# A fused attention and gated feed-forward kernel: first weight chunk loaded first, exponents guarded by a scaled absolute value, two buffers for the first product, and new planned times for the queues

## The chip, the cores and the metric

The kernel runs on one core of a Trainium2 chip. The metric is device time in microseconds (us) of one execution; smaller is better. Five engines work side by side, each through its own queue in order: TensorE (PE: matrix products; PEld is its loading of weights), VectorE (DVE), ScalarE (ACT), GpSimd (POOL), and SyncE (SP), which here issues all transfers (DMA) between the device memory and the on-chip memory.

## The reference

Attention over a causal window of 64 positions, then a feed-forward block with a gate that comes from a convolution over three positions:

```python
scores = scale * np.matmul(q, k.transpose(0, 1, 3, 2))      # 8 batches, 8 heads, 576 positions, 64 wide
mask = (rel >= 0) & (rel < 64)
scores = np.where(mask, scores, -1e9)
attn = np.exp(scores - scores.max(-1))
attn = attn / (attn.sum(-1) + 1e-09)
x = np.matmul(attn, v)                                      # heads side by side: 512 wide
h = np.maximum(x @ w_in, 0.0)                               # 512 -> 1024
conv_out = sum(conv_w[k] * hp[:, k:k + S] for k in range(3))
gate = 1 / (1 + np.exp(-conv_out))
out = (h * gate) @ w_out                                    # 1024 -> 512
```

q, k and v are float32; w_in, conv_w and w_out are float64.

## The kernel before

All 4608 positions (8 batches of 576) are cut into 12 units of 384 positions (NX), u = 0 to 11. For each unit the kernel computes:

- **scores**: twelve blocks in three batches b of four blocks each (`qk`), then the row maximum (`row_max`), the exponential (`exps`), a guard of the sums, a reciprocal and the normalising (`normalise`). In units 0 and 1 the blocks are 128 columns wide and TensorE transposes the result (`transpose_pe`, `untile`); from unit 2 on they are 96 wide, VectorE transposes, and transfers put the result in place.
- **values** (`values`, four column blocks c), split into a high part `xh` and a low part `xl` (`split_hi`, `split_lo`).
- **the first product** (`mm1`), for f = 0 to 7, blocks of 128 of the 1024 columns: three matmuls for high and low parts, for each of four c, so 12 calls for an f; then `relu` into `hbuf`.
- **the gate**: `conv_mid` on ScalarE, two `conv_side` on VectorE, `sig`, `gate`, `gate_hi` and `gate_lo`, for pairs of f.
- **the second product** (`mm2`), 12 calls for an f, into four accumulators `po`; at the unit's end these are copied and stored.

The weights come as float64 and are turned into a high and a low float32 part on the chip, once, in the first 100 us. They arrive as raw 32-bit words in chunks (`weights`, `to_f32`): ScalarE takes the absolute value of the high words (L248) and scales the low words (L255); GpSimd clamps at 2^-15 from below (L249, with TINY); VectorE shifts and masks (L250), puts the sign back (L252) and adds the low word (L256); then GpSimd (L273, for w_in) or ScalarE (L271, for w_out) rounds to the high part, and VectorE subtracts for the low part (L274). w_in comes as two chunks of one f and three of two, w_out as four of two.

The order of the instructions is made by a planner. Each piece of work is put on a list with `at(t, engine, cost, do, r, w)`: t is its planned place, in steps of one f (unit u starts at 8u), and r and w are what it reads and writes. `queued` goes through the list with costs written by hand and, for each engine, takes the ready piece with the smallest t. The instructions are then issued in that order, each engine's queue in order. So every number in the table START and every cost moves instructions on all queues. Where the planner sees TensorE idle in the first 110 us it puts in dummy matmuls on the zero tile `spare` (`keep_busy`, L212).

The raw words lie in a tile that is later used for the transposed scores and the output (`flat`, named T in the profile); `w24` (w in the profile) holds the converted chunk. `hbuf` is one buffer, so the relu of a unit must wait for the gate of the unit before.

Of the kernel before, what the change touches and what calls it, by code (L numbers as in the profile page):

```python
# [8 lines left out]
F32 = mybir.dt.float32  # L9
# [7 lines left out]
W = 64  # L17
# [11 lines left out]
LAG = 5  # L29
# [4 lines left out]
TINY = 2.0 ** -15  # L34
# [26 lines left out]
def queued(works, fill=None):  # L61
# [22 lines left out]
    free = {"PE": 0.0, "DVE": 0.0, "ACT": 2.0, "POOL": 0.7, "SP": 1.3}  # L84
    state = dict.fromkeys(free)
    waiting = {e: [] for e in free}
# [5 lines left out]
    while left:  # L92
# [17 lines left out]
        if fill and e == "PE" and start < FILL_TO:  # L110
            t = max(free[e], FILL_FROM)
            n = int((start - t) * FILL)
# [10 lines left out]
        if x.mb:  # L123
            dma = max(dma, start) + x.mb * 2.7
            end = dma + 1.9
        for k in x.r + x.w:
            if k in touched:
                touched[k] = e, end
# [12 lines left out]
    "v0": -34.213,  # L141
    "pv0": -15.486,
    "conv": -34.622,
    "bits": ((-44.162, -48.108), (-49.962, -46.523)),
    "qk1": -44.058,
    "v1": -6.318,
    "qk2": 0.918,
    "qk0": (-88.698, -55.197, -55.435),
    "ex0": (-38.484, -35.539, -25.91),
    "sc1": (-35.664, -14.916, -14.661),  # L150
    "ex1": (-10.948, -3.722, -2.234),
    "mask": -13.894,
    "sig": ((5.143, 6.743, 8.637, 10.624), (2.954, 4.077, 7.59, 9.996), (4.046, 6.806, 8.285, 10.314)),
    "in": (-40.063, -38.679, -33.327, -12.569, -5.818),
    "out": (-5.241, -4.847, 7.996, 9.148),
# [8 lines left out]
FILL, FILL_FROM, FILL_TO = 4.0, 2.0, 110.0  # L164
# [3 lines left out]
def attention_moe(ctx: ExitStack, tc: tile.TileContext, q, k, v, w_in, conv_w, w_out, out):  # L168
# [10 lines left out]
    hbuf = pool.tile([P, NF, NG + 2], F32, name="hbuf")  # L179
# [17 lines left out]
    bits = [flat.bitcast(U32)[:, 4 * DM * i:4 * DM * (i + 1)].rearrange("p (e two) -> p e two", two=2) for i in range(2)]  # L197
    T_BITS = (0,), (0, 1)
    w24 = many(2, [P, 2 * DM], F32, "w24")
# [26 lines left out]
    def load_qk(t, u, gs=(0, 1)):  # L226

        for g in gs:
            c, n = slice(2 * g, 2 * g + 2), (4, 2)[g] * W
            cut = (0, n + W, NX + W), (0, n, NX)  # L230
            for a in ((0, 1), (1, 2)) if u == 0 else ((0, 2),):
                for name, sb, dram, ends in (("k", ks, k, cut[0]), ("q", qs, q, cut[1])):
                    e = slice(ends[a[0]], ends[a[1]])
                    at(t, "SP", 0.7, lambda c=c, e=e, sb=sb, dram=dram: nc.sync.dma_start(sb[:, c, e], dram[u, :, c, e]),
                       w=[(name, g, i) for i in range(*a)], mb=0.00105 * (e.stop - e.start))

    def load_v(t, u):
        for g in range(2):
            c = slice(2 * g, 2 * g + 2)
            at(t, "SP", 0.7, lambda c=c: nc.sync.dma_start(vs[:, c], v[u, :, c]), w=[("v", g)], mb=0.79)  # L240
# [3 lines left out]
    def to_f32(t, n, st, x, kb, kt):  # L244
# [3 lines left out]
        at(t, "ACT", 0.0009 * n + 0.2, lambda: nc.scalar.activation(x, hw.bitcast(F32), AF.Abs), r=kb, w=kt)  # L248
        at(t, "POOL", 0.0027 * n + 0.02, lambda: nc.gpsimd.tensor_scalar(x, x, TINY, None, op0=ALU.max), w=kt, port=PORT_CL)  # L249
        two(t, "DVE", 0.00052 * n + 0.06, lambda: nc.vector.tensor_scalar(  # L250
            xu, xu, 3, 0x3FFFFFF8, op0=ALU.logical_shift_left, op1=ALU.bitwise_and), w=kt)
        two(t, "DVE", 0.00104 * n + 0.07, lambda: nc.vector.scalar_tensor_tensor(  # L252
            xu, hw, 0xC0000000, xu, op0=ALU.bitwise_and, op1=ALU.bitwise_or), r=kb, w=kt)
# [4 lines left out]
    def weights(t, src, fs, hi, lo, key, buf, halves):  # L258
# [4 lines left out]
        for f, a, tl in zip(fs, halves, load_at(buf, halves, t)):  # L263
            at(tl, "SP", 0.7, lambda f=f, a=a: nc.sync.dma_start(
                bits[buf][:, a * DM:(a + 1) * DM], src[f].bitcast(U32).rearrange("p (e two) -> p e two", two=2)),
               w=[("bits", buf, a)], mb=0.52)
        n = len(fs) * DM
        to_f32(t, n, st, x, kb, kt)
        his, los = [f"{key}{f}h" for f in fs], [f"{key}{f}l" for f in fs]
# [24 lines left out]
    def weights_conv(t_load, t):  # L294
        at(t_load, "SP", 0.7, lambda: nc.sync.dma_start(
# [40 lines left out]

# [397 lines left out]
```

## Time and profile before

| | us |
|---|---|
| median of 3 runs | 527.84 (527.21 to 528.04) |
| span of the profiled execution | 525.6 |
| PE busy | 516.8 (98%) |
| PEld busy | 499.1 (95%) |
| ACT busy | 384.7 (73%) |
| DVE busy | 377.9 (72%) |
| POOL busy | 105.2 (20%) |

The page gives no time for the profiled execution but its span, from the first to the last instruction; the runs' median is 2.2 us above it. The shares are averages over a prologue, in which weights are converted and the first scores are computed, and ten units or so that repeat at some 40 us each. A busy TensorE may be busy with dummy matmuls: these are told by their line, L212. The granted clock is 1.00 throughout.

### The profile page before, as it was taken

The page shows a single profiled execution, that of the slowest core. Times are in us where ns is not written, and L with a number is a line of the kernel's source. Part 1 is how long each engine was busy: PE and PEld are TensorE (multiplying, and loading weights), DVE is VectorE, ACT ScalarE, POOL GpSimd, SP SyncE. Part 2 cuts the span into 40 slices and gives each one's busy share as a digit, 9 for nine tenths or more (in the row PEclk, how much of TensorE's full clock was granted, in tenths as well). Part 3 has the DMA queues.
Part 4 walks back from the last instruction along what each step waited for, and adds up shares of the span by engine and source line. Part 5 has one row for each costly group of instructions (what it writes and reads, how often), then busy time and mean ns, then how long its engine had stood idle before and what let it go on. Part 6 is the DMA issues. An engine that isn't in the chain of part 4 may idle for free.

```text
span 525.6 us, 14814 instructions
## 1 busy us (share of the span) xinstructions
PE 516.8 (98%) x5814; PEld 499.1 (95%) x5814; DVE 377.9 (72%) x1084; ACT 384.7 (73%) x1017; POOL 105.2 (20%) x192
## 2 busy tenths in 40 slices
PE   9999899999999999999999999999999999999996
PEld 8988899999899999999999999999999999999996
DVE  3899999987667775677668667767767767645552
ACT  2999999796895984795795796697687687544541
POOL 6754663112120210120111011021021021000000
PEclk9999999999999999999999999999999999999999
DMA  8982850282472264272272173173083053010011
GB/s 285 382 287 92 265 221 1 72 304 81 136 253 54 68 218 117 68 275 64 67 268 68 61 259 76 44 289 78 16 301 85 10 178 83 13 61 0 2 60 61
DMA packets 29461, 69.97 MB, mean 133 GB/s; under 512 B 5712, under 2 KB 17616, under 8 KB 29392
## 3 DMA queue, kind: packets, MB, share of 16 engines
q1 hardware_dynamic: 29392, 69.03, 39.8%
q8 instruction: 46, 0.75, 0.6%
q14 instruction: 23, 0.19, 0.1%
HBM read 47.73 MB, written 9.47 MB: 109 GB/s over the span
## 4 chain that ended last, share of the span: by engine, by line
PE 90%; DVE 8%; issue 1%; ACT 0%
PE po L567 39%; PE acc L504 36%; PE acc L484 6%; PE sc L353 5%; PE acc L212 3%; DVE s L360 1%; DVE c L538 1%; DVE w L256 1%; DVE w L252 1%; DVE wil L274 1%; DVE s L381 1%; DVE w L250 1%; DVE xl L491 1%; PE po L353 0%; DVE cw L252 0%
## 5 line engine op out<-in xcount | busy, mean ns | idle before, releaser
L538 DVE SCALAR_TENSOR_TENSOR c<-hbuf,cw,c 128x386 f32<-128x386 f32 (+1 forms) x192 | 110.0, 624 | 32.9 <-ACT c L531 32.7
L567 PE MATMUL po<-gh,woh 128*128 128x386 f32 (+1 forms) x384 | 132.4, 345 | 0.0
L504 PE MATMUL acc<-xh,wih 128*128 128x384 f32 x384 | 131.1, 341 | 0.8 <-POOL sm L373 0.8
L567 PE MATMUL po<-gh,wol 128*128 128x386 f32 (+1 forms) x384 | 129.8, 338 | 0.0
L567 PE MATMUL po<-gl,woh 128*128 128x386 f32 (+1 forms) x384 | 129.8, 338 | 0.0
L504 PE MATMUL acc<-xh,wil 128*128 128x384 f32 x384 | 129.8, 338 | 0.0
L504 PE MATMUL acc<-xl,wih 128*128 128x384 f32 x384 | 129.7, 338 | 0.0
L370 ACT ACTIVATE s<-s,nm 128x96 f32<-128x96 f32 (+2 forms) x288 | 105.2, 369 | 6.5 <-DVE nm L360 6.3
L558 DVE TENSOR_TENSOR gl<-c,gh 128x772 fp32r<-128x772 f32 (+1 forms) x48 | 55.0, 1146 | 28.1 <-ACT gh L554 27.7
L567 PEld LDWEIGHTS po<-gh,woh 128*128 128x128 f32 x384 | 72.2, 188 | 2.9
L504 PEld LDWEIGHTS acc<-xh,wih 128*128 128x128 f32 x384 | 72.1, 188 | 2.4 <-POOL sm L373 1.0
L381 POOL TENSOR_TENSOR s<-s,r 128x768 f32<-128x768 f32 x27 | 39.7, 1471 | 165.6 <-DVE r L376 154.3
L550 DVE TENSOR_TENSOR c<-c,hbuf 128x772 f32<-128x772 f32 (+1 forms) x48 | 47.0, 981 | 35.9 <-ACT c L545 35.9
L567 PEld LDWEIGHTS po<-gl,woh 128*128 128x128 f32 x384 | 72.3, 188 | 0.0
L567 PEld LDWEIGHTS po<-gh,wol 128*128 128x128 f32 x384 | 72.3, 188 | 0.0
L504 PEld LDWEIGHTS acc<-xh,wil 128*128 128x128 f32 x384 | 72.2, 188 | 0.0
L504 PEld LDWEIGHTS acc<-xl,wih 128*128 128x128 f32 x384 | 72.1, 188 | 0.0
L525 ACT ACTIVATE hbuf<-acc 128x384 f32<-128x384 f32 x64 | 30.9, 486 | 44.6 <-PE acc L504 44.4
L545 ACT ACTIVATE c<-c 128x772 f32<-128x772 f32 (+1 forms) x48 | 40.7, 847 | 27.4 <-DVE c L538 27.2
L360 DVE CUSTOM_DVE_ANT_0 s<-sc,mask 128x96 f32<-128x96 f32 (+2 forms) x272 | 51.5, 255 | 11.0 <-POOL mask L321 7.0
L370 ACT ACTIVATION_READ_ACCUMULATOR s<-s,nm 128x1 f32 x288 | 54.7, 190 | 0.0
L531 ACT ACTIVATE c<-hbuf,cw 128x386 f32<-128x386 f32 (+1 forms) x96 | 53.6, 609 | 0.0
(64 smaller groups left out, 603.5 us busy)
## 6 DMA issues: line engine op xcount, KB each, us to landing
v<-in_v_dram SPq DMA_DIRECT2D x24, 768.0 KB, 7.3
ub<-T SPq DMA_DIRECT2D x240, 48.0 KB, 1.9
k<-in_k_dram SPq DMA_DIRECT2D x22, 448.0 KB, 5.3
q<-in_q_dram SPq DMA_DIRECT2D x22, 384.0 KB, 6.3
out_dram<-T SPq DMA_DIRECT2D x8, 772.0 KB, 4.4
T<-in_w_in_dram SPq DMA_DIRECT2D x8, 512.0 KB, 6.0
T<-in_w_out_dram SPq DMA_DIRECT2D x8, 512.0 KB, 5.3
out_dram<-T SPq DMA_DIRECT2D x3, 768.0 KB, 6.4
```

Source lines behind the costliest of these rows:

```text
L360: nc.vector.tensor_tensor_reduce(out=ss[b][:, i, h, o:n], in0=banks_of(u, b)[h][:, i * P + o:i * P + n], in1=mask[m][:, o:n], scale=-0.125 ...
L370: nc.scalar.activation(x, x, AF.Exp, bias=nms[b][:, e], scale=-1.0, accum_out=sms[b][:, e])
L381: on.tensor_tensor(sv, sv, rs[b].unsqueeze(2).broadcast_to([P, 2 * NB, n]), ALU.mult)
L484: nc.tensor.matmul(acc[bank(("v", u, c))][h * D:(h + 1) * D, t * W:(t + 1) * W], vs[:, c, t, h], ub[g][:, 2 * p:2 * p + 2, 2 * t + h], sta ...
L504: nc.tensor.matmul(acc[bank(("m", u, f))][:, :NX], w[:, f, c], x[u % 2][:, c], start=(c == 0 and j == 0), stop=(c == NC - 1 and j == 2))
L525: nc.scalar.activation(hbuf[:, f, o:o + NX], ps[:, :NX], AF.Relu)
L531: nc.scalar.activation(cs[i % 2][:, a, :n], hbuf[:, f, 1:1 + n], AF.Copy, scale=cw[:, 1, f:f + 1])
L538: nc.vector.scalar_tensor_tensor(c, hbuf[:, f, e:e + n], cw[:, e, f:f + 1], c, op0=ALU.mult, op1=ALU.add)
L545: nc.scalar.activation(c, c, AF.Sigmoid)
L550: nc.vector.tensor_tensor(c, c, hbuf[:, 2 * i:2 * i + 2, 1:1 + n], ALU.mult)
L558: nc.vector.tensor_tensor(gls[ring(u, i)][:, :, :n], cs[i % 2][:, :, :n], ghs[ring(u, i)][:, :, :n].bitcast(F32), ALU.subtract)
L567: nc.tensor.matmul(po[o][:, :n], w[:, f, es], x, start=(f == 0 and j == 0), stop=(f == NF - 1 and j == 2))
```

## The change

Four things are changed.

First, the conversion has no clamp any more: Abs gets a scale of 2^-112, and the shift and the sign are adapted, so that the chain goes from ScalarE to VectorE without GpSimd. Second, the raw words get a tile of their own (`bits`), and the converted chunks lie in T. Third, `hbuf` becomes two buffers, by u % 2. Fourth, the planner gets other rules and numbers: SyncE is taken as free from 0.75, an issue costs less, dummy matmuls are planned from 1.2 at 2.2 a microsecond up to the sixth, the scores and row maxima of wide blocks are planned in halves and blocks, the lag of the second product behind the first is a table instead of 5, and START is new nearly throughout; among it, the first chunk of w_in and the convolution's weights are loaded ahead of q and k.

```diff
-LAG = 5
-TINY = 2.0 ** -15
...
-    free = {"PE": 0.0, "DVE": 0.0, "ACT": 2.0, "POOL": 0.7, "SP": 1.3}
+    free = {"PE": 0.0, "DVE": 0.0, "ACT": 2.0, "POOL": 0.7, "SP": 0.75}
...
-            n = int((start - t) * FILL)
+            n = int((start - t) * (FILL if start > COLD else 2.2))
...
-    "bits": ((-44.162, -48.108), (-49.962, -46.523)),
+    "bits": ((-210.989, -90.898), (-76.132, -86.24)),
+    "lag": (5.734, 4.983, 5.01, 5, 4.601, 6.631),
...
-    hbuf = pool.tile([P, NF, NG + 2], F32, name="hbuf")
+    hbufs = many(2, [P, NF, NG + 2], F32, "hbuf")
...
-    bits = [flat.bitcast(U32)[:, 4 * DM * i:4 * DM * (i + 1)].rearrange("p (e two) -> p e two", two=2) for i in range(2)]
-    w24 = many(2, [P, 2 * DM], F32, "w24")
+    bits = many(2, [P, 2 * DM, 2], U32, "bits")
+    w24 = [flat[:, 8 * NT * 32:8 * NT * 32 + 2 * DM], flat[:, 16 * NT * 32:16 * NT * 32 + 2 * DM]]
...
-        at(t, "ACT", 0.0009 * n + 0.2, lambda: nc.scalar.activation(x, hw.bitcast(F32), AF.Abs), r=kb, w=kt)
-        at(t, "POOL", 0.0027 * n + 0.02, lambda: nc.gpsimd.tensor_scalar(x, x, TINY, None, op0=ALU.max), w=kt, port=PORT_CL)
-        two(t, "DVE", 0.00052 * n + 0.06, lambda: nc.vector.tensor_scalar(
-            xu, xu, 3, 0x3FFFFFF8, op0=ALU.logical_shift_left, op1=ALU.bitwise_and), w=kt)
+        at(t, "ACT", 0.0009 * n + 0.2, lambda: nc.scalar.activation(x, hw.bitcast(F32), AF.Abs, scale=2.0 ** -112), r=kb, w=kt)
+        two(t, "DVE", 0.00052 * n + 0.06, lambda: nc.vector.tensor_scalar(xu, xu, 3, None, op0=ALU.logical_shift_left), w=kt)
         two(t, "DVE", 0.00104 * n + 0.07, lambda: nc.vector.scalar_tensor_tensor(
-            xu, hw, 0xC0000000, xu, op0=ALU.bitwise_and, op1=ALU.bitwise_or), r=kb, w=kt)
+            xu, hw, 0x80000000, xu, op0=ALU.bitwise_and, op1=ALU.bitwise_or), r=kb, w=kt)
...
     def carry(u, fs):
+        hbuf = hbufs[u % 2]
...
-            nc.gpsimd.tensor_copy(hbuf[:, fs, :2], hbuf[:, fs, e:e + 2])
+            nc.gpsimd.tensor_copy(hbuf[:, fs, :2], hbufs[(u - 1) % 2][:, fs, e:e + 2])
...
-                at(n + LAG + 0.5 + 0.01 * o, "PE", 0.53, lambda f=f, o=o: mm2(u, f, o),
+                at(n + START["lag"][min(u, 5)] + 0.5 + 0.01 * o, "PE", 0.53, lambda f=f, o=o: mm2(u, f, o),
...
-    nc = bacc.Bacc("TRN2", target_bir_lowering=False, num_devices=1)
+    nc = bacc.Bacc("TRN2", target_bir_lowering=False, num_devices=1, dynamic_dma_scratch_size=1024)
```

The new code is longer, so lines get new numbers: dummy matmuls L212 become L214, scores L353 become L356, row maxima L360 become L363, the conversion's L248 and L250 become L250 and L251 (L252, L255, L256, L271, L273 and L274 keep theirs), normalising L381 becomes L384, transposes L387 become L390, values L484 become L495, the first product L504 becomes L515, the second L567 becomes L580.

How the order of the instructions moves, at three places, and by counts at a fourth. SyncE's queue at its start, before:

```order
L234 DMA k<-in_k_dram 128x2x320
L234 DMA q<-in_q_dram 128x2x256
L234 DMA k<-in_k_dram 128x2x128
L234 DMA q<-in_q_dram 128x2x128
L234 DMA k<-in_k_dram 128x2x192
...
L234 DMA k<-in_k_dram 128x2x256
L234 DMA q<-in_q_dram 128x2x256
L264 DMA T<-in_w_in_dram 128x1024 x4
```

and after:

```order
L264 DMA bits_102<-in_w_in_dram 128x1024
L295 DMA cbits<-in_conv_w_dram 128x48
L236 DMA k<-in_k_dram 128x2x320
L236 DMA q<-in_q_dram 128x2x256
L236 DMA k<-in_k_dram 128x2x128
...
L236 DMA q<-in_q_dram 128x2x256
L264 DMA bits_102<-in_w_in_dram 128x1024
L264 DMA bits_103<-in_w_in_dram 128x1024 x2
```

One chunk of w_in and the convolution's weights stand ahead of the first k and q; the other three chunks stay behind these.

VectorE's queue from the first batch's reciprocal on, in unit 0 (s_80 and s_81 are the first two batches before), before:

```order
L250 TENSOR_SCALAR w_101<-w_101 128x512
L252 SCALAR_TENSOR_TENSOR w_101<-T,w_101 128x512
L376 RECIPROCAL r_89<-sm_86 128x8
L381 TENSOR_TENSOR s_80<-s_80,r_89 128x1024
L250 TENSOR_SCALAR w_101<-w_101 128x512
L256 ISA w_101<-T,w_101 128x1024
L252 SCALAR_TENSOR_TENSOR w_101<-T,w_101 128x512
...
L256 ISA w_101<-T,w_101 128x1024
L274 TENSOR_TENSOR wil<-w_101,wih 128x512
L376 RECIPROCAL r_90<-sm_87 128x8
L381 TENSOR_TENSOR s_81<-s_81,r_90 128x1024
L274 TENSOR_TENSOR wil<-w_101,wih 128x512
```

and after (where these batches are s_81 and s_82; the first chunk's L251 and L252 stand at the very front of the queue, its L256 and L274 between the first row maxima):

```order
L379 RECIPROCAL r_90<-sm_87 128x8
L256 ISA cw<-cbits,cw 128x48
L384 TENSOR_TENSOR s_81<-s_81,r_90 128x1024
L251 TENSOR_SCALAR T<-T 128x512
L379 RECIPROCAL r_91<-sm_88 128x8
L252 SCALAR_TENSOR_TENSOR T<-bits_102,T 128x512
L384 TENSOR_TENSOR s_82<-s_82,r_91 128x1024
L256 ISA T<-bits_102,T 128x1024
L274 TENSOR_TENSOR wil<-T,wih 128x512
```

The second batch's normalising has moved ahead of the row maxima of unit 1, and L274 of the second chunk stands right behind its L256, with the rounding L273 on GpSimd between them.

TensorE's queue where unit 0 is transposed for the first time, before:

```order
L212 MATMUL acc_106<-spare 128x112 x28
...
L387 MATMUL po_108<-ident,s_80 128x128 x4
L387 MATMUL po_109<-ident,s_80 128x128 x4
L212 MATMUL acc_106<-spare 128x112 x8
...
L212 MATMUL acc_106<-spare 128x112 x7
L387 MATMUL po_110<-ident,s_81 128x128 x4
L387 MATMUL po_111<-ident,s_81 128x128 x4
L212 MATMUL acc_106<-spare 128x112 x3
L484 MATMUL acc_106<-ub_61,v 64x64 x12
```

(sixteen scores of unit 1 stand in each of the two gaps) and after:

```order
L214 MATMUL acc_107<-spare 128x112 x15
L390 MATMUL po_109<-ident,s_81 128x128 x4
L390 MATMUL po_110<-ident,s_81 128x128 x4
L214 MATMUL acc_107<-spare 128x112 x3
L390 MATMUL po_111<-ident,s_82 128x128 x4
L390 MATMUL po_112<-ident,s_82 128x128 x4
L214 MATMUL acc_107<-spare 128x112 x3
L495 MATMUL acc_107<-ub_61,v 64x64 x12
```

The scores of unit 1 have moved behind the first values. Over the whole queue there are 99 dummy calls before and 63 after; ahead of the first scores there are 12 before and 20 after.

TensorE's queue where the second product for f = 6 and 7 of unit 0 begins has, ahead of that place, 174 calls of the first product, 96 of the values and 128 narrow scores (four batches of 32) before, and 180, 120 and 160 after.

151 lines of the change are left out of this document (84 added, 67 removed), and 6 rows, old and new, of the table START.

## The prediction

> **What bounds the kernel now.** I read the stages first, then TensorE's waits, then the dummy matmuls, then VectorE up to the last converted weight. The columns of the stage rows are length, then busy time of PE, PEld, DVE, ACT and POOL, granted clock, DMA share, GB/s.
>
> ```profile
> 0.00:36.71 36.71, 34.70 (x536) 32.44 (x537) 26.92 (x120) 26.52 (x100) 23.86 (x62) 1.00 0.88 317
> 36.71:65.44 28.73, 26.34 (x358) 24.40 (x358) 28.70 (x67) 26.58 (x64) 14.41 (x10) 1.00 0.59 194
> 65.44:113.60 48.16, 48.04 (x527) 46.66 (x524) 46.05 (x124) 43.01 (x100) 15.52 (x20) 1.00 0.38 124
> 234.00:274.40 40.40, 40.40 (x483) 39.07 (x482) 28.57 (x88) 30.55 (x83) 5.77 (x11) 1.00 0.40 132
> ```
> ```profile
> PE sc L353 <- DVE nm L360: 1.3, 2, 0.9
> PE acc L212 <- DVE spare L215: 1.0, 1, 1.0
> PE po L387 <- DVE s L381: 0.9, 2, 0.7
> PE acc L504 <- POOL sm L373: 0.8, 1, 0.8
> PE acc L484 <- DVE xl L491: 0.5, 1, 0.5
> ```
> From the third stage on TensorE is busy nearly without a gap, and a unit in the middle has no gap at all: there the arithmetic of TensorE alone sets the time, and VectorE and ScalarE have a quarter free. All waits of TensorE, 4.5 us, lie before 65.44. In the second stage VectorE is busy for 28.70 of 28.73 us. So the prologue is set by VectorE, and TensorE fills its holes with dummy matmuls (L212), which look busy and are worth nothing:
>
> ```profile
> 0.00:65.44 65.44, 27.40 (x198) 25.66 (x198) 1.00 0.75 263
> 1.05 5.46 PE L212 MATMUL acc<-spare 128*128 128x112 f32 x24 [1.05 <-DVE spare L215]
> 6.44 1.38 PE L353 MATMUL sc<-k,q 64*64 64x64 f32 x32
> 7.75 1.15 PE L212 MATMUL acc<-spare 128*128 128x112 f32 x8
> 11.64 6.50 PE L212 MATMUL acc<-spare 128*128 128x112 f32 x56
> 44.37 1.16 PE L353 MATMUL sc<-k,q 64*32 64x96 f32 x64 [0.32 <-DVE nm L360]
> 55.62 1.62 PE L484 MATMUL acc<-ub,v 128*64 128x64 f32 x48
> 97.48 5.81 PE po L567 x33
> 118.90 2.13 PE po L567 x12
> ```
> Only what TensorE does in vain, 27.40 + 4.5 = 31.9 us, can be won. The question is how early VectorE lets it stop. The last thing that VectorE must give is the low half of the last output-weight chunk (L274, at 95.54 below); TensorE needs it for the row at 97.48, the second product for f = 6 and 7 of the first unit, before which stand 72 calls of that product.
>
> **The sum, on VectorE.** I counted the instructions that the order puts up to that L274. Before and after they are the same kinds and counts but for three: 8 more row maxima of 96 columns, one normalising of 768 columns and one reciprocal fewer. So VectorE's time to this point changes by its start, by its waits, and by how long the same instructions take.
>
> ```profile
> 0.00:96.67 96.67, 85.71 (x241) 1.00 0.61 212
> 8.00 0.23 DVE L360 CUSTOM_DVE_ANT_0 s<-sc,mask 128x64 f32<-128x64 f32 x1 [7.00 <-POOL mask L321]
> 14.54 0.43 DVE L250 TENSOR_SCALAR w<-w 128x512 uint32<-128x512 uint32 x1 [1.00 <-POOL w L249]
> 16.06 1.52 DVE L381 TENSOR_TENSOR s<-s,r 128x1024 f32<-128x1024 f32 x1
> 22.37 1.40 DVE L381 TENSOR_TENSOR s<-s,r 128x1024 f32<-128x1024 f32 x1
> 28.68 2.06 DVE L381 TENSOR_TENSOR s<-s,r 128x1024 f32<-128x1024 f32 x1
> 40.62 1.22 DVE L381 TENSOR_TENSOR s<-s,r 128x1024 f32<-128x1024 f32 x1
> 21.54 0.69 DVE L274 TENSOR_TENSOR wil<-w,wih 128x512 fp32r<-128x512 f32 x1
> 23.69 1.52 DVE L274 TENSOR_TENSOR wil<-w,wih 128x512 fp32r<-128x512 f32 x1
> 57.22 0.68 DVE L250 TENSOR_SCALAR w<-w 128x1024 uint32<-128x1024 uint32 x1
> 62.87 1.21 DVE L250 TENSOR_SCALAR w<-w 128x1024 uint32<-128x1024 uint32 x1
> 52.53 0.24 DVE L360 CUSTOM_DVE_ANT_0 s<-sc,mask 128x96 f32<-128x96 f32 x1
> 53.95 1.14 DVE L538 SCALAR_TENSOR_TENSOR c<-hbuf,cw,c 128x386 f32<-128x386 f32 x2
> 39.45 1.02 DVE L252 SCALAR_TENSOR_TENSOR cw<-cbits,cw 128x24 uint32<-128x24 uint32 x1
> 95.54 1.22 DVE L274 TENSOR_TENSOR wol<-w,woh 128x1024 fp32r<-128x1024 f32 x1
> 27.90 3.50 POOL L249 TENSOR_SCALAR w<-w 128x1024 f32<-128x1024 f32 x1 [1.17 <-ACT w L248]
> 18.59 1.00 POOL L273 CAST wih<-w 128x512 fp32r<-128x512 f32 x1 [1.20 <-DVE w L256]
> 12.24 0.68 ACT L248 ACTIVATE w<-T 128x512 f32<-128x512 f32 x1 [3.21 <-DMA T<-in_w_in_dram]
> ```
> - **The clamp leaves GpSimd** (one of 3.50 us stands above). VectorE ran on beside it, but some instructions were drawn out: the normalisings by 0.30, 0.18 and 0.84 against 1.22, L274 by 0.83, L250 by 0.53, and the tiny L252 by some 0.9. That is 3.6 us, plus the wait of 1.00 at 14.54. The scale in ScalarE's Abs makes no new instruction, and one arithmetic step fewer in L250 I price at 0; if the row went by steps it would be at most half of 0.68 in each, some 2.5 us over the nine.
> - **The first chunk comes first.** Its steps L250 and L252 on VectorE (some 1.3 us with the small ones for the convolution) move into the time ahead of the row maxima, in which VectorE waited 7 us. ScalarE's wait of 3.21 goes too.
> - **The first scores come later.** Twenty dummy calls stand ahead of them instead of twelve. Each call is two rows: twelve took 5.39 (1.05 to 6.44), and the next went at 1.07 for four (7.75 to 8.82), so twenty end at 1.05 + 5.39 + 2.14 = 8.6. The chunk and the small load push q back, but not beyond that:
>
> ```profile
> 1.24 0.46 SPq L234 DMA_DIRECT2D q<-in_q_dram  x1
> q<-in_q_dram SPq DMA_DIRECT2D x1, 256.0 KB, 3.4
> T<-in_w_in_dram SPq DMA_DIRECT2D x1, 512.0 KB, 6.2
> T<-in_w_in_dram SPq DMA_DIRECT2D x1, 512.0 KB, 6.9
> ```
>   q landed at 4.6. Two issues of half a microsecond and one chunk (the second of two issued 0.5 apart lands 1.2 later) put it at some 6.9. With about 1.0 for the scores at the later rate and the 0.25 that passed from 7.75 to 8.00, the row maxima start at 9.8 instead of 8.00.
> - **A new wait.** For the second chunk L256 and L274 now stand next to each other, with GpSimd's L273 (1.00) between them: VectorE waits some 1.3 us, and its row maxima stand behind it. Before, other work stood there. Bounds: 0 (if VectorE is late anyway) and 2.6 (both small chunks); I take 1.3.
>
> Busy time without the first memset (0.17) is 85.5; it becomes 85.5 - 3.6 - 1.3 + 0.4 = 81.0. The 0.4 is 1.4 for eight row maxima (52.53 to 53.95) less some 1.0 for the small normalising (three quarters of 1.22) and the reciprocal. VectorE's other waits between 8.00 and 96.67 were 88.67 - 85.54 - 1.00 = 2.1; I keep them and add 1.3. The last low half is then ready at 9.8 + 81.0 + 3.4 = 94.2 instead of 96.7.
>
> **The sum, on TensorE.** By its row at 97.48 TensorE had done 174 calls of the first product, 72 of the second, 96 of the values and four score batches of 32 calls. With the second h buffer the order lets unit 1 run further ahead: ahead of the same row stand 180, 72, 120 and five. That is 3.7 us of useful work more (6 calls at 2.13 for twelve; 24 calls of the values, 48 rows, at 1.55, since what follows the row at 55.62 starts at 57.17; a batch at 1.1). TensorE gets there at 94.2 + 0.2 = 94.4 instead of 97.48, so it is 97.48 - 94.4 + 3.7 = 6.8 us ahead. The same from the other side: 99 dummy calls become 63, of which 20 cost 7.5 and 43 at 6.43 / 28 cost 9.9, so 17.4 instead of 27.4; of the 10.0 saved, 3.2 come back as waits on VectorE that nothing fills.
>
> **What costs nothing.** From 65.44 TensorE waits for nothing, so the new lags and places of units 2 and later reorder a full engine: 0 either way, with up to a microsecond lost if a half comes late. The copies across the two h buffers and one more small memset lie on GpSimd, busy 5.77 of 40.40. GpSimd issues no transfer of data in the trace, so the smaller scratch for its descriptors changes nothing but room. The end (after 521.3) is unchanged.
>
> The page gives 525.6 us of span for the profiled execution and no other time; the median of the runs lies 2.2 above it. The forecast is 527.84 - 6.8 = 521.0.
>
> **A rule against the trace.** The POOL row at 27.90 lasts 3.50 us, and in it VectorE's L381 took 2.06 instead of 1.22. The Trainium skill, page SBUF — State Buffer, section Who interferes with whom, has it that a GpSimd instruction and a VectorE instruction with two SBUF inputs exclude each other for the whole of the one that came first. By that rule L381 could not end before 31.40; the trace has it end at 30.74, so the lock is not whole here. By the rule each of nine clamps would hold VectorE for its length, the time would fall by far more, and the third rival below would be the case.
>
> **Rivals.**
> 1. VectorE gains little: its waits grow from 3.4 to 6 or 7, since the row maxima hang on scores which TensorE, in order, issues behind transposes and values that wait for VectorE again. For it: the list of waits runs both ways. Against it: in the second stage VectorE had 0.03 us without work. Then 97.5 for the last half, and 527.84 - (97.48 - 97.7 + 3.7) = 524.4.
> 2. Slower. The first scores are 2.1 us later (8.6 for 6.44), and everything of the softmax chain with them; if the clamps had cost VectorE only what it had to spare, nothing pays that back, and the cast adds 1.3. The price is 2.1 + 1.3 = 3.4, so 531.2. It decides where the normalising of the third batch of unit 0 starts later than 28.68 + 2. Against it: the wait of 1.00 and the 0.84 lie on just that chain.
> 3. VectorE is freed further, and TensorE is bound by its own order: waits of VectorE vanish, or the clamps' cost was larger. TensorE's useful work to its row is 65.6 + 3.7 = 69.3; with 17.4 of dummies and 1.05 at the start it gets there at 87.7, and the time is 527.84 - (97.48 - 87.7 + 3.7) = 514.4. Half way from the forecast, 517.7, is likelier.
>
> **Chances.** Forecast (gain of 3.6 to 9.8) 0.72, first rival 0.10, third 0.10, no change 0.03, slower 0.05. Two tenths of a per cent, 1.05 us, is about what this kernel's runs (527.21 to 528.04) can tell from no change. Faster is 0.92, same 0.03, slower 0.05. The range takes the forecast's bounds, 527.84 - 9.8 = 518.0 and 527.84 - 3.4 = 524.4: waits of VectorE of 0.4 and 6.8.
>
> **What would show it.** The first scores at 8.5 to 8.8 and the first row maximum near 9.8; no L249 on GpSimd; normalisings of 1024 columns within 1.3; an L274 of 512 columns waiting for L273; L212 at 17 to 18 us in all; the last low half at 92 to 96; a middle unit still at 40.2. Wrong would be a wait of TensorE after 100, or row maxima that wait for scores by more than 2 us in sum.

## The result, and the profile after

The changed kernel takes 520.0 us (median of 4 runs, 519.84 to 520.37) against 527.91 for the kernel before (4 runs, 527.21 to 528.04): a ratio of 0.9845, interval 0.9812 to 0.9878. That is 7.9 us less; 6.8 were forecast. The profiled execution took 519.87 us, its span is 517.9 us, and before's was 525.6. One execution of e12_rows_in_line below took 1271.6 us and is left out of all its numbers.

The stages of after, cut as those of before (length, then busy time of PE, PEld, DVE, ACT and POOL, granted clock, DMA share, GB/s):

```profile
0.00:36.71 36.71, 33.16 (x457) 30.14 (x458) 25.71 (x123) 28.19 (x106) 16.04 (x57) 1.00 0.87 311
36.71:65.44 28.73, 27.16 (x466) 24.49 (x466) 27.97 (x85) 25.48 (x61) 7.50 (x18) 1.00 0.71 266
65.44:113.60 48.16, 47.41 (x513) 44.94 (x513) 46.31 (x107) 41.23 (x84) 5.38 (x13) 1.00 0.32 96
234.00:274.40 40.40, 40.40 (x484) 39.07 (x483) 27.29 (x87) 30.04 (x83) 6.13 (x11) 1.00 0.41 136
```

The picture is the same as before: TensorE has no gap in a middle unit, and VectorE has few in the second stage. GpSimd fell from 23.86 to 16.04 and from 14.41 to 7.50 us. What TensorE does in vain is next, the dummies (now L214), then the start of the program and the row that needs the last low half:

```profile
0.00:65.44 65.44, 18.31 (x126) 16.50 (x126) 1.00 0.80 291
```
```profile
1.05 6.24 PE L214 MATMUL acc<-spare 128*128 128x112 f32 x40 [1.05 <-DVE spare L217]
7.21 1.00 PE L356 MATMUL sc<-k,q 64*64 64x64 f32 x32
...
95.13 0.45 PE L580 MATMUL po<-gh,woh 128*128 128x386 f32 x1
```

The dummies fell from 27.40 to 18.31 us. The second product for f = 6 and 7 starts at 95.13. The prediction's 97.48 for before is the time at which the chain of work takes that row over, and by the chain after's is 95.20; in before's timeline the row is

```profile
97.32 0.34 PE L567 MATMUL po<-gh,woh 128*128 128x386 f32 x1
```

So it comes 2.2 us earlier, with 3.7 us more of useful work done ahead of it. VectorE, by its timeline (start, length, line; in brackets the wait ahead of it) and by its waits from 8.3 to 95.2 us (in all, times, longest):

```profile
5.07 0.53 DVE L251 TENSOR_SCALAR T<-T 128x512 uint32<-128x512 uint32 x1 [4.08 <-ACT T L250]
...
8.38 0.23 DVE L363 CUSTOM_DVE_ANT_0 s<-sc,mask 128x64 f32<-128x64 f32 x1 [1.87 <-PE sc L356]
...
19.48 0.69 DVE L274 TENSOR_TENSOR wil<-T,wih 128x512 fp32r<-128x512 f32 x1 [0.71 <-POOL wih L273]
...
22.20 0.29 DVE L363 CUSTOM_DVE_ANT_0 s<-sc,mask 128x128 f32<-128x128 f32 x1 [2.03 <-PE sc L356]
...
25.28 1.22 DVE L384 TENSOR_TENSOR s<-s,r 128x1024 f32<-128x1024 f32 x1
...
93.95 1.22 DVE L274 TENSOR_TENSOR wol<-T,woh 128x1024 fp32r<-128x1024 f32 x1
```
```profile
DVE s L363 <- PE sc L356: 5.3, 4, 2.0
DVE c L563 <- ACT c L558: 1.8, 2, 1.5
DVE wil L274 <- POOL wih L273: 0.7, 1, 0.7
DVE xl L502 <- ACT xh L499: 0.4, 1, 0.4
DVE T L251 <- ACT T L250: 0.2, 1, 0.2
```

The first chunk's L251 lies ahead of the row maxima, the normalising takes 1.22 instead of 1.22 to 2.06, and the last low half is ready at 95.2 instead of 96.8. The 5.3 us of waiting for scores hold the 1.87 ahead of the first row maximum.

### The profile page after: what moved, and what is told of

Its sections match the earlier page's. It is cut to its first block, busy times and chain, and to the rows that moved or that the text cites. A ratio compares the mean times of both kernels' runs of the same rounds, so it can differ in the third digit from the quotient of the medians.

```text
span 517.9 us, 14661 instructions
## 1 busy us (share of the span) xinstructions
PE 508.0 (98%) x5742; PEld 488.4 (94%) x5742; DVE 372.4 (72%) x1084; ACT 382.8 (74%) x1015; POOL 85.4 (16%) x186
## 4 chain that ended last, share of the span: by engine, by line
PE 82%; DVE 9%; DMA 5%; ACT 1%; issue 1%; SPq 1%; ACTq 0%
PE po L580 38%; PE acc L515 33%; PE acc L495 6%; PE sc L356 5%; DMA q<-in_q_dram 2%; DVE s L363 2%; DMA bits<-in_w_out_dram 1%; DVE s L384 1%; DVE T L252 1%; DVE T L256 1%; DMA k<-in_k_dram 1%; DVE c L563 1%; DVE wil L274 1%; DVE xl L502 1%; SPq L236 1%
## 5 line engine op out<-in xcount | busy, mean ns | idle before, releaser
L580 PE MATMUL po<-gh,woh 128*128 128x386 f32 (+1 forms) x384 | 132.4, 345 | 0.0
L515 PE MATMUL acc<-xh,wih 128*128 128x384 f32 x384 | 130.7, 340 | 0.6 <-ACT hbuf L534 0.6
L580 PE MATMUL po<-gh,wol 128*128 128x386 f32 (+1 forms) x384 | 130.0, 339 | 0.0
L580 PE MATMUL po<-gl,woh 128*128 128x386 f32 (+1 forms) x384 | 129.7, 338 | 0.1
L515 PE MATMUL acc<-xh,wil 128*128 128x384 f32 x384 | 129.0, 336 | 0.3 <-issue 0.3
L515 PE MATMUL acc<-xl,wih 128*128 128x384 f32 x384 | 128.8, 335 | 0.0
L551 DVE SCALAR_TENSOR_TENSOR c<-hbuf,cw,c 128x386 f32<-128x386 f32 (+1 forms) x192 | 111.9, 633 | 22.5 <-ACT c L544 22.4
L580 PEld LDWEIGHTS po<-gh,woh 128*128 128x128 f32 x384 | 72.2, 188 | 2.9
L515 PEld LDWEIGHTS acc<-xh,wih 128*128 128x128 f32 x384 | 72.1, 188 | 2.7 <-ACT hbuf L534 1.1
L580 PEld LDWEIGHTS po<-gl,woh 128*128 128x128 f32 x384 | 72.4, 188 | 0.4 <-DVE gl L571 0.4
L515 PEld LDWEIGHTS acc<-xh,wil 128*128 128x128 f32 x384 | 72.1, 188 | 0.5 <-issue 0.5
L580 PEld LDWEIGHTS po<-gh,wol 128*128 128x128 f32 x384 | 72.2, 188 | 0.0
L515 PEld LDWEIGHTS acc<-xl,wih 128*128 128x128 f32 x384 | 72.1, 188 | 0.0
L571 DVE TENSOR_TENSOR gl<-c,gh 128x772 fp32r<-128x772 f32 (+1 forms) x48 | 51.8, 1082 | 22.1 <-ACT gh L567 21.8
L384 POOL TENSOR_TENSOR s<-s,r 128x768 f32<-128x768 f32 x27 | 40.4, 1496 | 152.1 <-DVE r L379 138.8
L363 DVE CUSTOM_DVE_ANT_0 s<-sc,mask 128x96 f32<-128x96 f32 (+2 forms) x272 | 51.9, 257 | 16.8 <-PE sc L356 16.8
L567 ACT CAST gh<-c 128x772 fp32r<-128x772 f32 (+1 forms) x48 | 40.0, 834 | 18.4 <-DVE c L563 13.7
```

Source lines behind the costliest of these rows:

```text
L363: nc.vector.tensor_tensor_reduce(out=ss[b][:, i, h, o:n], in0=banks_of(u, b)[h][:, i * P + o:i * P + n], in1=mask[m][:, o:n], scale=-0.125 ...
L384: on.tensor_tensor(sv, sv, rs[b].unsqueeze(2).broadcast_to([P, 2 * NB, n]), ALU.mult)
L515: nc.tensor.matmul(acc[bank(("m", u, f))][:, :NX], w[:, f, c], x[u % 2][:, c], start=(c == 0 and j == 0), stop=(c == NC - 1 and j == 2))
L551: nc.vector.scalar_tensor_tensor(c, hbufs[u % 2][:, f, e:e + n], cw[:, e, f:f + 1], c, op0=ALU.mult, op1=ALU.add)
L567: nc.scalar.copy(ghs[ring(u, i)][:, :, :n], cs[i % 2][:, :, :n])
L571: nc.vector.tensor_tensor(gls[ring(u, i)][:, :, :n], cs[i % 2][:, :, :n], ghs[ring(u, i)][:, :, :n].bitcast(F32), ALU.subtract)
```

## The experiments

All ratios are to the kernel before on the same chip, whose median was 527.9 to 528.2 us.

| kernel | us, median (range) | ratio (95%) |
|---|---|---|
| e4_before_no_clamp | 526.27 (525.89 to 530.69) | 0.9986 (0.9965 to 1.0006) |
| e1_clamp_back | 534.35 (533.52 to 536.00) | 1.0121 (1.0099 to 1.0144) |
| e5_clamp_planned | 530.58 (529.30 to 534.99) | 1.0047 (1.0023 to 1.0071) |
| e2_kq_first | 525.22 (523.08 to 527.88) | 0.9939 (0.9917 to 0.9961) |
| e3_one_h | 523.24 (523.02 to 523.53) | 0.9908 (0.9893 to 0.9922) |
| e7_low_on_gpsimd | 524.09 (523.55 to 524.44) | 0.9913 (0.9889 to 0.9938) |
| e9_no_later_dummies | 519.88 (519.03 to 522.77) | 0.9846 (0.9815 to 0.9877) |
| e10_ten_first | 519.94 (518.31 to 522.30) | 0.9841 (0.9808 to 0.9874) |
| e6_pad | 526.38 (525.29 to 527.02) | 0.9957 (0.9940 to 0.9975) |
| e11_shift_128 | 520.78 (520.00 to 522.86) | 0.9856 (0.9830 to 0.9881) |
| e12_rows_in_line | 524.67 (524.54 to 525.63) | 0.9934 (0.9910 to 0.9958) |
| e13_both | 525.75 (525.18 to 527.55) | 0.9954 (0.9932 to 0.9977) |

**The clamp alone (e4_before_no_clamp).** The kernel before in its own order, with the scaled Abs and without the clamp's instruction.

```diff
-        at(t, "ACT", ..., lambda: nc.scalar.activation(x, hw.bitcast(F32), AF.Abs), ...)
-        at(t, "POOL", ..., lambda: nc.gpsimd.tensor_scalar(x, x, TINY, None, op0=ALU.max), ...)
+        at(t, "ACT", ..., lambda: nc.scalar.activation(x, hw.bitcast(F32), AF.Abs, scale=2.0 ** -112), ...)
+        at(t, "POOL", ..., lambda: None, ...)
```

> The kernel before with its own order of all queues, but without the clamp: Abs has the scale, and shift and sign are as in the changed kernel. Theory (99 dummy matmuls stand in TensorE's queue and cost 27 us whatever VectorE does; only the waits of 4.5 us can shrink): VectorE reaches the last low half 3 to 5 us earlier, but the time falls by 1 to 3 us only, to 525 to 527. Rival (the clamp alone is the gain): 519 to 521.

It came to 526.27, some 1.7 us below before, with an interval that reaches just past no change. VectorE's groups in the first 100 us (busy, mean ns) are these, first of e4_before_no_clamp, then of before:

```profile
L381 DVE TENSOR_TENSOR s<-s,r 128x1024 f32<-128x1024 f32 (+1 forms) x9 | 10.3, 1147 | 0.1
L274 DVE TENSOR_TENSOR wil<-w,wih 128x1024 fp32r<-128x1024 f32 (+1 forms) x5 | 5.0, 1003 | 0.0
```
```profile
L381 DVE TENSOR_TENSOR s<-s,r 128x1024 f32<-128x1024 f32 (+1 forms) x9 | 11.5, 1274 | 0.1
L274 DVE TENSOR_TENSOR wil<-w,wih 128x1024 fp32r<-128x1024 f32 (+1 forms) x5 | 5.8, 1168 | 0.0
```

The drawing out is gone as forecast, 1.2 and 0.8 us in these two groups, but the last low half starts at 94.69 instead of 95.54 only. Even these 0.85 us come from the start: the first dummies took 4.71 us instead of 5.46, and the first row maximum is at 6.86 instead of 8.00. From there to the last low half it is 87.8 us, and 87.5 in before. So in the old order the time won turns into other waits, and the theory's 3 to 5 us on VectorE did not come; its range for the time was met all the same. What the 1.7 us consist of is not shown.

**The clamp in the new order (e1_clamp_back, e5_clamp_planned).** In the first it is issued at ScalarE's place in an order that knows nothing of it; in the second it is a step of its own and the whole order is planned round it.

```diff
+        def magnitude():                                            # e1
+            nc.scalar.activation(x, hw.bitcast(F32), AF.Abs, scale=2.0 ** -112)
+            nc.gpsimd.tensor_scalar(x, x, 0.0, None, op0=ALU.max)
+        at(t, "POOL", 0.0027 * n + 0.02, lambda: nc.gpsimd.tensor_scalar(x, x, 0.0, None, op0=ALU.max), w=kt, port=PORT_CL)   # e5
```

> The changed kernel, with GpSimd's clamp back behind each of ScalarE's Abs instructions (here a maximum with 0, which changes no value); every queue else keeps its order. Theory (VectorE is the bound up to the last converted weight, and the clamp drew its instructions out): VectorE's busy time up to the last low half rises by 2 to 4 us, the second chunk's L251 waits for the clamp, and the time is 3 to 5.5 us above the changed kernel, 523 to 525.5. Rival (the new order alone brought the gain, the clamp ran in time that VectorE and GpSimd had to spare): at most 1 us above it, under 521.

It missed both: 534.35, 14.3 over after. VectorE's waits of e1_clamp_back and a stage of it show why (its lines from L252 on stand four further):

```profile
DVE T L255 <- POOL T L252: 10.1, 3, 6.6
DVE r L383 <- POOL sm L380: 6.7, 3, 3.0
```
```profile
40.00:60.00 20.00, 17.18 (x300) 15.39 (x299) 15.94 (x66) 15.35 (x49) 8.11 (x10) 0.83 0.40 134
```

VectorE stands 10.1 us in three places for the clamp, and 6.7 for the guard of the sums, which on GpSimd stands behind it. The longest of the three, 6.6, lies at the start, where after's VectorE stands 4.1 for the chunk as well. TensorE then runs out of work that its dummies don't cover, and its granted clock falls to 0.83.

> The kernel after with a maximum with 0.0 on GpSimd behind each magnitude (it changes no value), entered as a step of its own, so that the whole order is planned round it; in e1_clamp_back it stood in an order that did not know of it and cost 14.3 us. Theory: what the clamp costs of itself is what it draws out and makes VectorE wait, 4.6 us at the bound; the other 10 us of e1_clamp_back were VectorE and TensorE standing behind steps that came later than the order supposed. Planned round it, the kernel takes 523.5 to 526.5 us, VectorE's first row maxima stay ahead of 9 us, and the waits for POOL T come to less than 6 us (10.1 there). Rival: 14 us are the clamp's price in any order that starts the weights this early, 530 us or more.

Planned round it, the clamp costs 10.6 instead of 14.3 us. The rival's number was met, the theory's was not; its wait for the clamp was gone, but not the time. In e5_clamp_planned the first row maximum and the last low half lie at

```profile
9.46 0.23 DVE L364 CUSTOM_DVE_ANT_0 s<-sc,mask 128x64 f32<-128x64 f32 x1 [8.47 <-PE sc L357]
...
102.20 1.21 DVE L275 TENSOR_TENSOR wol<-T,woh 128x1024 fp32r<-128x1024 f32 x1
```

The first row maximum is 1.1 us later, which is not the clamp: the dummies ahead of the first scores took 7.31 us instead of 6.24. But the first chunk's steps on VectorE now stand behind the first row maxima (at 11.02), and the planner put the last chunk behind one pair of the gate more, so that the last low half starts 8.3 us later than after's. The table START was made for an order without the clamp; a table made for one with it wasn't tried. What the two runs and e4_before_no_clamp show together: without the clamp the rest of the change gains 6.3 us (526.27 to 520.0); with it, in the better of the two ways, the rest loses 2.7 (527.9 to 530.58).

**The first chunk (e2_kq_first).** The order of after, with the eight transfers of q and k moved to the front of SyncE's queue.

```diff
-        for x in queued(plan, keep_busy):
+        order = queued(plan, keep_busy)
+        first = [x for x in order if x.eng == "SP" and x.w and x.w[0][0] in "qk"][:8]
+        for x in first + [x for x in order if x not in first]:
```

> The changed kernel, with the first eight loads of k and q put ahead of the first weight chunk and of the convolution's weights on SyncE's queue; nothing else moves. Theory (first chunk first is worth something only because the queues of ScalarE and VectorE have its steps ahead of the first row maximum): the chunk lands near 11 us instead of 5, VectorE's first row maximum starts near 12 instead of 8.4, and the time is 2.5 to 4 us longer, 522.5 to 524. Rival (the early chunk is hidden, the scores would start earlier instead): within 0.5 us of the changed kernel or below it.

525.22: 5.2 over after, the theory's direction and a microsecond more. In its timeline of VectorE

```profile
11.86 0.43 DVE L251 TENSOR_SCALAR T<-T 128x512 uint32<-128x512 uint32 x1 [10.87 <-ACT T L250]
...
13.03 0.22 DVE L363 CUSTOM_DVE_ANT_0 s<-sc,mask 128x64 f32<-128x64 f32 x1
...
99.62 1.22 DVE L274 TENSOR_TENSOR wol<-T,woh 128x1024 fp32r<-128x1024 f32 x1
```

the row maxima stand behind the first chunk's L251, which waits until 11.86; all 4.65 us of that later start, and 1 more, are found at the last low half.

**The second buffer (e3_one_h).**

```diff
-    hbufs = many(2, [P, NF, NG + 2], F32, "hbuf")
+    hbufs = many(1, [P, NF, NG + 2], F32, "hbuf") * 2
...
-        n0, x, y = NF * u, u % 2, u % 2
+        n0, x, y = NF * u, u % 2, 0
```

> The changed kernel with one h buffer for all units, planned anew by the same rules, so that a unit's relu waits for the gate of the unit before. Theory (the second buffer lets TensorE do the next unit's first product while VectorE is late): TensorE gets waits or dummies of some 2 to 4 us back between 60 and 100 us, and the time is 522 to 524. Rival (the order has other work to put there, the buffer is worth nothing): 520 to 520.7.

523.24, inside the theory's range, 3.2 over after. One wait of TensorE, 0.6 in after, has grown:

```profile
PE acc L515 <- ACT hbuf L534: 2.1, 1, 2.1
```

That is 1.5 us, less than the theory's 2 to 4, so its number was met in part by luck. The rest is mostly not a wait: the first product's matmuls are slower throughout, by 1.0 ns each in the table below, which is 1.2 us for 1,152. This led to the next three.

**Where the weights lie (e6_pad, e11_shift_128, e12_rows_in_line).** From the traces' start times I took the mean distance of one matmul to the next, after 120 us: over some 860 pairs of the first product, 250 of the second with 384 columns and 640 with 386. "Weights" and "gh" are where the tiles start in each partition, beyond a multiple of 256 bytes.

| kernel | weights | gh rows | first, ns | second 384 | second 386 |
|---|---|---|---|---|---|
| before | 0 | several | 175.97 | 175.95 | 176.39 |
| e3_one_h | 0 | several | 175.86 | 176.41 | 176.26 |
| after | 128 | several | 174.86 | 175.44 | 176.44 |
| e6_pad | 128 | several | 174.85 | 175.21 | 176.44 |
| e11_shift_128 | 0 | several | 175.83 | 176.28 | 176.28 |
| e12_rows_in_line | 128 | 128 | 174.18 | 173.70 | 176.22 |

```diff
+    pad = pool.tile([P, NF, NG + 2], F32, name="pad")        # e6, in before, with the smaller scratch of after
+    pad = pool.tile([P, 32], F32, name="pad")                # e11, in after
+    shift = pool.tile([P, 16], F32, name="shift")            # e12, beside e6's pad
+    ghs, gls = many(3, [P, 2, 448], F32R, "gh"), many(3, [P, 2, 448], F32R, "gl")
```

> The kernel before with an unused tile of the size of one buffer of the first product's results, which stands ahead of the weights' tiles and moves their addresses by its size; nothing in the program reads or writes it, and every instruction stays. Theory: the first product's matmuls start 174.8 ns apart in the kernel after and 176.0 in the kernel before because the weights lie at other addresses; then this one shows 174.7 to 175.0 ns and takes 526.3 to 526.8 us (1,152 calls by 1.2 ns are 1.4 us less than 528.0). Rival: the second buffer helps by the order in which it is written and read; then 175.8 to 176.1 ns and 527.6 to 528.4 us.

526.38 and 174.85 ns: an unused tile makes the first product 1.1 ns quicker a matmul, and the kernel 1.6 us. The same is seen in the groups (busy, mean ns), of before, of e6_pad, and of e11_shift_128, where the shift back takes it away:

```profile
L504 PE MATMUL acc<-xl,wih 128*128 128x384 f32 x308 | 103.9, 337 | 0.0
```
```profile
L505 PE MATMUL acc<-xl,wih 128*128 128x384 f32 x308 | 103.2, 335 | 0.0
```
```profile
L516 PE MATMUL acc<-xl,wih 128*128 128x384 f32 x317 | 107.0, 338 | 0.0
```

> The kernel after with an unused tile of 128 bytes a partition ahead of the weights' tiles. The start of the w_in high halves in each partition is 62848 in the kernel after, 65792 in the kernel before and 50432 in e3_one_h; in multiples of 256 bytes that is 245.5, 257 and 197, and the two whole ones are the two slow ones. Here it is 62976, 246 times 256, with everything from there on 128 bytes further. Theory: what counts is where the weights lie against a line of 256 bytes (or against the moving operand, which lies half a line off in all of these); then the first product goes back to 175.8 to 176.1 ns a matmul and the kernel takes 521.2 to 521.8 us. Rival: it is the region of the memory, not the line; then 174.8 ns and 519.7 to 520.5 us.

175.83 ns: 128 bytes decide, not the region. The time, 520.78, lies between the two theories' ranges, and its spread (520.00 to 522.86) does not separate it from after. The traces do. TensorE's 5742 matmuls stand in the same order in both; those of e11_shift_128 are 1.1 us behind after's at 113 us, and 2.4 us behind at 489 us. The 1.1 us come from the start, where its dummies took 7.79 us instead of 6.24; the 1.3 us are lost evenly on the way and are what the theory asked for.

> e6_pad with the gate's tiles gh and gl, the second product's moving operands, in rows of 448 instead of 386 elements and an unused 64 bytes ahead of them, so that every row starts half a line of 256 bytes off, as the first product's moving operands do and as all weights do in e6_pad; the same instructions on the same number of elements. Theory: a matmul's start-to-start time depends on both operands' places against the line; the second product, at 176.1 ns in e6_pad, comes to 174.7 to 175.3 ns and the kernel to 524.7 to 525.4 us (1,152 calls by 0.8 to 1.4 ns below 526.4). Rival: the second product is slow for another reason (386 elements instead of 384, four accumulators in turn), and stays at 176.0 to 176.3 ns, 526.1 to 526.7 us.

524.67, at the lower end of the theory's range, but by another sum: the second product of 384 columns gained 1.5 ns and the first one 0.7, though nothing of it was moved; the one of 386 gained 0.2. Why the two columns more keep it at 176.2 is open. In e6_pad and e11_shift_128 all tiles behind the weights move with them, and here a matmul gains whose own operands stay. So it is shown that the places count, and not that the weights' own place is the cause.

**VectorE as the bound (e7_low_on_gpsimd).** The order of after, with the four low halves of w_out on GpSimd.

```diff
+        on = nc.gpsimd if key == "out" else nc.vector
-        two(t, "DVE", ..., lambda: nc.vector.tensor_tensor(lo, x, hi.bitcast(F32), ALU.subtract), ...)
+        two(t, "DVE", ..., lambda: on.tensor_tensor(lo, x, hi.bitcast(F32), ALU.subtract), ...)
```

> The kernel after with the four w_out low halves (L274, 1024 elements each, 1.22 us on VectorE) computed by GpSimd at the same places of the order. Theory: VectorE bounds the prologue, so what is taken from it arrives at the second product: its work ahead of the last low half is 3.7 us less, and the last half itself takes some 2.0 us on GpSimd (1.50 us for 768 elements of the normalising, scaled) instead of 1.22, so that it is ready at 91.5 to 93.5 us instead of 95.1 and the kernel takes 517.0 to 518.5 us. Rival 1: GpSimd and VectorE draw each other out, the VectorE instructions beside the four low halves take longer by as much, 519.5 to 521 us. Rival 2: TensorE is held by its stand-ins and not by VectorE, 520 us with a TensorE that waits no less.

524.09: rival 1, and more of it than was expected. The first of the four and what stood beside it on VectorE, in e7_low_on_gpsimd (lines one further); a like pair of instructions in after:

```profile
61.13 2.40 POOL L275 TENSOR_TENSOR wol<-T,woh 128x1024 fp32r<-128x1024 f32 x1 [0.80 <-ACT woh L271]
```
```profile
60.60 3.34 DVE L552 SCALAR_TENSOR_TENSOR c<-hbuf,cw,c 128x386 f32<-128x386 f32 x2
```
```profile
59.85 1.14 DVE L551 SCALAR_TENSOR_TENSOR c<-hbuf,cw,c 128x386 f32<-128x386 f32 x2
```

3.34 instead of 1.14: the pair lost 2.2 us beside a subtraction of 2.40. The other three met such instructions too: the 19 of L552 that stand up to 96 us took 1060 ns in the mean instead of 615.

```profile
L552 DVE SCALAR_TENSOR_TENSOR c<-hbuf,cw,c 128x386 f32<-128x386 f32 x19 | 19.3, 1060 | 0.0
```

VectorE gave away 4 x 1.22 = 4.9 us and lost 19 x 0.445 = 8.5, and the row of the second product moved from 95.13 to 96.68. Of these 1.55 us the start has a part that no subtraction touches: the first dummies took 7.29 us instead of 6.24, and the first row maximum is 1.05 later. By TensorE's start times, against those of the same matmuls in after, another 1.9 us are lost between 99 and 105 us. By the section Who interferes with whom of the Trainium skill's page SBUF — State Buffer, a VectorE instruction with two SBUF inputs and a GpSimd instruction that reads SBUF exclude each other; these rows agree, where the clamp's row in the prediction (2.06 beside 3.50) did not.

**The dummies (e9_no_later_dummies, e10_ten_first).** All but the first 20 left out; or 10 first ones.

```diff
-            n = int((start - t) * (FILL if start > COLD else 2.2))
+            n = int((start - t) * FILL) if start < 8 else 0              # e9
+            n = int((start - t) * (FILL if start > 8 else 2.0))          # e10
```

> The kernel after without the stand-in matmuls of L214 but for the first 20 (43 groups' 106 calls or so left out); they compute nothing that is used. Theory: VectorE holds the prologue, so the stand-ins lie in time in which TensorE would wait anyway and taking them away brings nothing by itself: 519.5 to 520.5 us if the granted clock stays at 1.00, with 15 to 17 us more of waiting in the list of waits. Rival 1: they delay TensorE's own work, by up to a stand-in's length at each group; 517 to 519 us. Rival 2: they hold the clock, which falls in the stretch from 20 to 65 us as it fell to 0.83 in e1_clamp_back; then 521 to 526 us.

519.88, in the median no different from after. The granted clock fell where the dummies had been (the column ahead of the last two), and TensorE waited openly:

```profile
0.00:20.00 20.00, 12.82 (x152) 11.76 (x152) 12.08 (x64) 13.65 (x54) 12.03 (x52) 0.87 0.92 334
20.00:40.00 20.00, 15.15 (x296) 12.91 (x295) 16.35 (x73) 17.64 (x66) 3.66 (x6) 0.96 0.81 291
```
```profile
PE po L390 <- DVE s L384: 7.5, 3, 4.8
```

The 12 us of busy time that went left the median where it was: TensorE was not the bound there. That the dummies do neither good nor harm is not shown, for two small effects may cancel. In the trace the last low half starts at 92.39 instead of 93.95, and that execution took 519.03 us. The two of the six with the lowest mean clock, 0.982, took 522.16 and 522.77 us; the other four, at 0.992 to 0.993, took 519.03 to 520.04.

> The kernel after with 10 instead of 20 stand-in matmuls ahead of the first scores; nothing else. In the kernel after the first scores start at 7.21 us, right behind the last of the 20. Theory: the scores wait for the first halves of k and q and the stand-ins end no later than these land, so the first scores start at 6.9 to 7.3 us and the first row maxima within 0.3 us of 8.38; 519.6 to 520.5 us. Rival: the stand-ins hold them; then the first scores start near 4.5 us, the first row maxima near 6 us, and what VectorE bounds comes earlier by 1 to 2 us, 518 to 519.2 us.

In e10_ten_first the first scores and the first row maximum are at

```profile
7.19 1.77 PE L356 MATMUL sc<-k,q 64*64 64x64 f32 x32 [1.53 <-DMA q<-in_q_dram]
```
```profile
9.12 0.23 DVE L363 CUSTOM_DVE_ANT_0 s<-sc,mask 128x64 f32<-128x64 f32 x1 [2.83 <-PE sc L356]
```

The scores wait for q until 7.19, as the theory said; they then take 1.77 instead of 1.00 us, and the first row maximum is 0.74 late. The time, 519.94, does not show it: later waits of VectorE are shorter by as much.

**Both together (e13_both).** e9_no_later_dummies with e12_rows_in_line's rows; for want of room gl has two buffers.

```diff
+    ghs, gls = many(3, [P, 2, 448], F32R, "gh"), many(2, [P, 2, 448], F32R, "gl")
```

> The kernel after with the two things that e9_no_later_dummies and e12_rows_in_line did apart: no stand-ins but the first 20, and gh and gl in rows of 448 elements half a line of 256 bytes off; gl has two buffers instead of three, for room. Theory: the gains by place are the same in this order as in before's, 0.7 ns a first-product matmul, 1.5 ns a second-product matmul of 384 elements and 0.2 ns one of 386, together 1.0 to 1.5 us, and the third gl buffer was not needed: 518.3 to 519.2 us against 519.9 of e9_no_later_dummies. Rival: gl's two buffers make VectorE's last subtraction of a pair wait for the second product of two pairs before, in the units' changes above all, which gives the gain back: 519.6 to 521 us and a new wait for PE po at the gate's low half.

525.75, the rival, and more. The matmuls are quicker (174.26, 173.97 and 176.17 ns), but TensorE now waits in the middle units, which are full in after:

```profile
PE po L581 <- DVE gl L572: 4.9, 7, 0.8
```

In this order the third buffer of gl is needed. These waits are 4.9 of the 5.9 us over e9_no_later_dummies; where the rest and the gain of the quicker matmuls went was not followed. A version with all three and the padded rows has no room in this layout and wasn't tried, so none of the kernels is clearly faster than after.

## Why the prediction was right

The likeliest case came true: VectorE bounds the prologue, gets through it sooner, and the second product for f = 6 and 7 moves. In its own steps:

- **The start** was mis-sized for this execution. Twenty dummies end at 7.2 and not at 8.6 (6.2 us, not 7.5), and the first row maximum is at 8.38 instead of 9.8. But the same twenty calls took 6.24 to 7.79 us in the nine traces that begin with them, and after's is the shortest; the longest is that of e11_shift_128:

```profile
1.05 7.79 PE L215 MATMUL acc<-spare 128*128 128x112 f32 x40 [1.05 <-DVE spare L218]
```

  So the 7.5 lies inside of what this instruction sequence does, and after's early start is luck. q landed at 7.2 (e10_ten_first), near the 6.9 of the estimate.
- **VectorE's busy time** held: 95.1 - 8.38 less 6.5 of waits is 80.2, forecast 81.0.
- **Its waits** were mis-sized the other way: 5.3 - 1.87 + 1.8 + 0.7 + 0.4 + 0.2 = 6.5 instead of 3.4. Of that, 3.4 are row maxima that wait for scores, at 22.20 (2.03), 24.31 and 29.55. This is the first rival's mechanism, and the sign set for "wrong", over 2 us, was met. The new wait behind L273 was 0.7, forecast 1.3.
- Start and waits cancelled, so **the last low half** is ready at 95.2, forecast 94.2. That they cancelled is luck too: in e11_shift_128, where the same order starts its row maxima at 9.93, the row comes at 96.24. TensorE is (97.32 - 95.13) + 3.7 = 5.9 us ahead there, not 6.8.
- **That this half holds TensorE** is not shown. In neither trace does TensorE stand idle just ahead of the row. In before the half is ready at 96.8, and the first product runs on without a gap until 97.3; in after the half is ready at 95.2, just as the row begins. The last waits of TensorE in the lists lie earlier: at 64.60 for the split of the values on VectorE (L491) in before, at 56.83 for the same step (L502) and at 58.47 for a load of q in after. The chain of work that ended last leaves VectorE at 64.55 in before (L491) and at 89.45 in after (L571, the low part of a gate), in neither at a half of the weights. So VectorE does set the prologue's end, but through other steps than the one that the prediction's sum ran to.
- **"From 65.44 on 0 either way" failed.** The trace's end is 7.7 us earlier, so by this sum 1.8 were won after that row. 972 calls of the first product still come, each 1.1 ns quicker, which is 1.1 us; e6_pad and e11_shift_128 show that this is the place of the weights and of the tiles behind them, moved by the second buffer. Some 0.7 us is not accounted for.
- **The other side of the sum** comes out closer. The dummies fell to 18.31, forecast 17.4, so 9.1 us were saved; TensorE's waits in the lists rose from 4.5 to 5.7, so 1.2 came back where 3.2 were forecast. The difference, 7.9, is the whole gain. Over the whole trace, with each moment counted once, the first product is 0.7 us shorter and TensorE's other useful work as much longer, so that the quicker matmuls add nothing on balance.
- **The clamp's price** of 4.6 us was not what its removal gains. Alone it gains some 1.7 (e4_before_no_clamp), which is not clear of no change. As far as e1_clamp_back and e5_clamp_planned show, its worth is that the early first chunk and the new order stand on it: the three parts that were undone one by one cost 3.2, 5.2 and 14.3 us, and do not add up to 7.9. The fourth part, the planner's new numbers, was not undone alone, so its own share is open.
- The second rival's condition, a third normalising later than 30.68, did not come: it is at 25.28. Against the third rival, a TensorE bound by its own order, stands e9_no_later_dummies: with 12 us less to do, TensorE ended no earlier in the median.

## What to carry to other kernels

Taking an instruction off a shared queue may gain little where it stood and still be what allows an earlier order; measure it alone and within the new order, since the two answers can lie far apart (1.7 and 10.6 us here). Dummies can look like 18 us of work and be no bound: take them out before calling the engine the bound. Two traces can differ by a microsecond from their start alone, so compare them from the same event on as well. And when a buffer is added, compare the matmuls' start-to-start time before and after, for the addresses of everything behind it have moved.

## What had not been expected of the hardware

- 128 bytes in the start of the weights' tiles, and of all tiles behind them, change a first-product matmul by 1.1 ns: it took 175.8 to 176.0 ns in before, e3_one_h, e4_before_no_clamp and e11_shift_128, and 174.7 to 174.9 in after, in e6_pad and in the six other kernels with the tiles of after. The kernel e6_pad is 1.6 us faster than before. Where the moving rows were put in the same place too, it was 173.7 to 174.2. What in the memory does it is open.
- GpSimd's 2.40 us subtraction of two tiles stretched two VectorE instructions from 1.14 to 3.34 us; its clamp, with one input and 3.50 us, had drawn out a normalising by 0.84 only. GpSimd's spans are rough in the profile, so its two lengths are too.
- Without the later dummies the granted clock of the first 20 us was 0.87 and that of the next 0.96, and the median time was the same. TensorE had time to spare there; that it lost none by the clock is not shown.
- The same twenty dummy calls at the start took 6.24 to 7.79 us in nine traces, with the granted clock shown as 1.00 in all of them. On what this depends is open.
